# Windowed attention and a feed-forward layer on one core: TensorE in program order, one piece of weights converted per step, and the first loads in another order

## The chip, the cores and the metric

The kernel runs on one core of one Trainium2 chip. The metric is the device time of one execution in microseconds (us), from the first to the last instruction and what lies around them; the kernel before took 915.77 us as the median of three runs (915.74 to 917.31). A profile is one such execution taken by the hardware profiler, and its times count from the start of the span.

## What is computed

Eight batches of eight heads attend over 576 positions with a head dimension of 64. Heads 0 to 3 see the 32 positions that end at their own (the plain window), heads 4 to 7 see 32 positions that are four apart (the dilated window). The 4608 rows of 512 that this gives go through a feed-forward layer with 2048 inner columns. Everything is in float32.

```
scores = q @ k^T / sqrt(64), outside the window -1e9
attn   = exp(scores - max) / (sum + 1e-9)
x      = (attn @ v), heads side by side      # 4608 x 512
h      = x @ w_in                            # 512 x 2048
g      = h * clip(h + 3, 0, 6) / 6
out    = g @ w_out                           # 2048 x 512
```

## The kernel before

**The feed-forward layer** is cut into 12 chunks `c` of 384 rows and 16 slices `f` of 128 inner columns, so there are 192 steps (c, f). To keep the accuracy of float32, each matrix is split into a high and a low part (`xh` and `xl`, `gh` and `gl`, two parts of each weight in `wt`), and a product is three matmuls: high by high, high by low, low by high. The *first product* of a step (`gemm1`, lines 407 to 409) is 12 matmuls of 128x384 into one of two buffers `ps_h`. ScalarE (L412) and VectorE (L413) make g of it, ScalarE rounds it to its high part `gh` (L416), and VectorE subtracts that to get the low part `gl` (L417). The *second product* (`gemm2`, lines 428 to 430) is 9 matmuls of 128x512 into three accumulators `ps_o`; it belongs to the step two earlier (`LAG`). The accumulators are three of the six buffers `ps_a`, and the attention has the other three from the first second product on.

The steps do not run chunk by chunk from the start: they begin with (0,0) to (0,3), then alternate between chunk 0 and chunk 1, (0,4), (1,0), (0,5), (1,1) and so on, and from chunk 2 on they go chunk by chunk. Step 5 is therefore (1,0), the first to need rows of chunk 1.

**The attention** is done in 48 *trios*, each a group of blocks of 32 queries that fills 128 rows. The first 12 (`NFIRST`) run in rounds `tau` = 0 to 15, written in `first_items`: round tau does the scores of trio tau with the values of trio tau-3 mixed among them (`st_both`, on TensorE L228, L163 and L173), turns (transposes on TensorE, L242, and a copy on ScalarE, L247) the exponentials `e` of trio tau-1 and the result `x` of trio tau-4, and splits the latter into `xh` (ScalarE, L299) and `xl` (GpSimd, L302). The softmax is VectorE's (L195 and the lines around it) and so is the normalising by the sum (`z`, L207 and L208). From trio 9 on the values are single 32x65 matmuls that the trace shows in groups. The other 36 trios are set beside steps of the layer by a table (`beside`).

**The weights** come as 32 pieces, two per slice f (one of w_in, one of w_out), in 512 KB each (L323). They are 64-bit words and have to be put together to float32 on the chip in three stages, and one piece passes one stage per *beat* (`convert_beat`): *fields* (ScalarE twice, L338 and L339, VectorE L340), *join* (VectorE L346 and L350, then ScalarE's cast to the high part, L351) and *split* (VectorE L355 for the low part). A beat does the split of piece p-2, the join of piece p-1 and the fields of piece p. The beats ahead of the steps are set by the table `CB`, which lists the rounds in which one is run. From step 4 to step 29 (`LEAD` to `BEATS`) `step_at` runs one beat per step, and at even steps (`EXTRA` = 2) a second one at the end of the step.

**The loads** of q, k, v and the weights all stand on SP's queue, in the order in which they are written at the end of the function. `WITH` says how many pieces of weights are asked for after the loads of each round. The first nine trios have their loads in buffers of the weights' pool (18 buffers), the later ones in a pool of three, so that these wait for the trio three before. ScalarE's queue has the loads of the results out; GpSimd issues none.

**The order of the work.** `turn_of` gives what follows it a priority, in steps of the layer, and a scheduler orders the instructions of each engine by that and by what it thinks each will take. The order in which TensorE does the products, the small matmuls of the attention and the turns is therefore the scheduler's, and differs from the order in which the code is written. The lines that count most are:

```
        turn_of(n + 0.4)
        if LEAD <= n < BEATS:
            convert_beat()
        turn_of(n + G2)
        if n >= LAG:
            gemm2(*steps[n - LAG])
        ...
        turn_of(n + 0.9)
        if LEAD <= n < BEATS and n % EXTRA == 0:
            convert_beat()
```

Of the kernel before, what the change touches and what calls it, by code (L numbers as in the profile page):

```python
# [23 lines left out]
SPARE = 2  # L24
WORK = 12
BEATS = 30
EXTRA = 2
WARM = 8
ONV = ()
AHEAD = 3  # L30
LEAD = 4
NFIRST = 12
NLOAD = 3
NWIDE = 9
WITH = (0, 0, 0, 0, 2, 0, 2, 0, 2, 2, 2, 2)
CB = (6, 6, 7, 7, 8, 8, 9, 9, 10, 10, 11, 11, 12, 12)
BASE = 8
CD = 0.5
EARLY = (8, 9, 10, 11, 12, 13, 14, 15, 15)
# [7 lines left out]
def windowed_attention_ffn(ctx: ExitStack, tc: tile.TileContext, qk, vp, w, mask, out):  # L47
# [79 lines left out]
    def load_tile(t, name, at, n):  # L127

        if t >= NWIDE:
            return loads.tile([P, n], F32, name=name, tag=name)  # L130
        if t not in wide:
            wide[t] = wpool.tile([P, 4, DM], F32, name="first", tag="w").rearrange("p a n -> p (a n)")
        return wide[t][:, at : at + n]

    def load_qk(t):
        if t < T and t not in kqs:
            kqs[t] = load_tile(t, "kq", 0, KW + CH)
            nc.sync.dma_start(out=kqs[t], in_=qk[t].rearrange("h d x -> (h d) x"))

    def load_v(t):  # L140
        if t < T and t not in vs:
            v = load_tile(t, "v", KW + CH, TB * W)
            vs[t] = v.rearrange("p (n x) -> p n x", x=W)
            nc.sync.dma_start(out=v, in_=vp[t].rearrange("h k x -> (h k) x"))
# [176 lines left out]
    def load_w(p):  # L321
        st = wpool.tile([P, 4, WN], F32, name="st", tag="w")
        pace(nc.sync.dma_start(  # L323
            out=st[:, 0:2].rearrange("p a n -> p (a n)").bitcast(U32), in_=w[p // 2, p % 2].bitcast(U32)
        ))
        staged[p] = st
# [7 lines left out]
    def cv_fields(p):  # L334
        if p % 2 == 0:
            wt[p // 2] = wpool.tile([P, 4, WN], F32R, name="wt", tag="w")
        hi_w, lo_w, v, a, _, _ = parts(p)
        pace(nc.scalar.mul(v, hi_w, 2.0**-112))  # L338
        pace(nc.scalar.mul(a.bitcast(U32), lo_w.bitcast(U32), 2.0**-29))  # L339
        nc.vector.tensor_scalar(  # L340
            out=v.bitcast(U32), in0=v.bitcast(U32), scalar1=3, scalar2=None, op0=ALU.logical_shift_left
        )

    def cv_join(p):
        hi_w, _, v, a, hi, _ = parts(p)
        nc.vector.scalar_tensor_tensor(  # L346
            out=v.bitcast(U32), in0=hi_w.bitcast(U32), scalar=0x80000000, in1=v.bitcast(U32),
            op0=ALU.bitwise_and, op1=ALU.bitwise_or,
        )
        nc.vector.tensor_tensor(out=v.bitcast(U32), in0=v.bitcast(U32), in1=a.bitcast(U32), op=ALU.add)  # L350
        nc.scalar.copy(hi, v)  # L351

    def cv_split(p):
        _, _, v, _, hi, lo = parts(p)
        nc.vector.tensor_tensor(out=lo, in0=v, in1=hi.bitcast(F32), op=ALU.subtract)  # L355
        del staged[p]
# [5 lines left out]
    def load_ahead(n):  # L362
        while beat["loaded"] < min(n, NP):
            f = beat["fields"] // 2
            if len(staged) + f + 1 + 1 > NF + SPARE and len(staged) > 0 and beat["loaded"] >= 2:
                break
            load_w(beat["loaded"])
            beat["loaded"] += 1

    def convert_beat():  # L370
        if beat["split"] < beat["join"]:
            cv_split(beat["split"])
            beat["split"] += 1
        if beat["join"] < beat["fields"]:
            cv_join(beat["join"])
            beat["join"] += 1
        p = beat["fields"]
        if p < NP:
            load_ahead(p + 1)
            if p < beat["loaded"]:  # L380
                cv_fields(p)
                beat["fields"] += 1
        load_ahead(p + AHEAD)
# [10 lines left out]
    def turn_of(n):  # L394
        tc.cur_priority = max(first[0] + int(n * STEP), 0) + 1000

    def gemm1(n, c, f):
        last["g"] = True
        weights_ready(f)
        assert all(x in written for x in trios if c in chunks(*x))  # L400
        read[c] += 1
        r0 = (c * CH) % (2 * S)
        ph = ps_h.tile([P, CH], F32, name="ps_h")
        for kt in range(NK):
            a, b = xh[:, kt, r0 : r0 + CH], xl[:, kt, r0 : r0 + CH]
            ks = slice(kt * P, (kt + 1) * P)
            nc.tensor.matmul(ph, lhsT=wt[f][:, 0, ks], rhs=a, start=(kt == 0), stop=False)  # L407
            nc.tensor.matmul(ph, lhsT=wt[f][:, 0, ks], rhs=b, start=False, stop=False)  # L408
            last["pe"] = nc.tensor.matmul(ph, lhsT=wt[f][:, 1, ks], rhs=a, start=False, stop=(kt == NK - 1))  # L409
        turn_of(n + EV)  # L410
        t = work_tile("t")
        nc.scalar.activation(t, ph, AF.Relu, bias=three, scale=1.0)  # L412
        nc.vector.scalar_tensor_tensor(out=t, in0=t, scalar=6.0, in1=ph, op0=ALU.min, op1=ALU.mult)  # L413
        gh = work_tile("gh", F32R)
        gl = work_tile("gl", F32R)
        nc.scalar.copy(gh, t)  # L416
        nc.vector.tensor_tensor(out=gl, in0=t, in1=gh.bitcast(F32), op=ALU.subtract)  # L417
        gs[c, f] = gh, gl

    def gemm2(c, f):  # L420
        gh, gl = gs.pop((c, f))
        if f == 0:
            po[c] = [ps_a.tile([P, DM], F32, name="ps_o", tag="ps_a") for _ in range(TT)]
        if f == NF - 1:
            o = wpool.tile([P, TT, DM], F32, name="o", tag="w")
        for tt in range(TT):
            ts = slice(tt * P, (tt + 1) * P)
            nc.tensor.matmul(po[c][tt], lhsT=gh[:, ts], rhs=wt[f][:, 2], start=(f == 0), stop=False)  # L428
            nc.tensor.matmul(po[c][tt], lhsT=gh[:, ts], rhs=wt[f][:, 3], start=False, stop=False)  # L429
            last["pe"] = nc.tensor.matmul(po[c][tt], lhsT=gl[:, ts], rhs=wt[f][:, 2], start=False, stop=(f == NF - 1))  # L430
            if f == NF - 1:
                nc.scalar.mul(o[:, tt], po[c][tt], 1.0 / 6.0)
                r = c * CH + tt * P
                nc.scalar.dma_start(out=out[r : r + P, :], in_=o[:, tt])
# [31 lines left out]
    for i, p in enumerate(at):  # L466
        t = NFIRST + i
# [7 lines left out]
    def step_at(n):  # L475
        c, f = steps[n] if n < len(steps) else (None, None)
        turn_of(n)
        if c is not None:
            gemm1(n, c, f)
        turn_of(n + DEL)  # L480
        for step in beside.get((c, f, 0), []):
            step()
# [6 lines that stand above are left out]
        turn_of(n + DEL + 0.5)  # L489
        for step in beside.get((c, f, 1), []):  # L490
            step()
        turn_of(n + 0.9)
        if LEAD <= n < BEATS and n % EXTRA == 0:
            convert_beat()

    first[0] = BASE * STEP
    some = P + 2 * CH
# [3 lines left out]
    load_qk(1)  # L501
    load_qk(2)
    nc.sync.dma_start(out=mi[:, some:], in_=mask[:, some:])
    load_v(0)
    for t in range(3, NFIRST + 2):
        if t < NFIRST:
            load_qk(t)
        load_v(t - 2)
        load_ahead(sum(WITH[: t - 1]))
    n = 0  # L510
    for tau in range(NFIRST + 4):
        turn_of(tau - BASE)
        first_items(tau)
        turn_of(tau - BASE + CD)
        for _ in range(CB.count(tau)):
            convert_beat()
        for _ in range(EARLY.count(tau)):
            step_at(n)
            n += 1
    while n < len(steps) + LAG:  # L520
        step_at(n)
        n += 1
# [92 lines left out]
```

## Time and profile before

| what | value |
|---|---|
| median of three runs | 915.77 us (915.74 to 917.31) |
| the profiled execution | 915.34 us |
| its span, first to last instruction | 913.6 us (1.7 us lie around it) |
| mean granted TensorE clock | 0.991 |
| TensorE busy | 891.0 us, 98% |
| VectorE busy | 444.0 us, 49% |
| ScalarE busy | 346.5 us, 38% |
| GpSimd busy | 62.5 us, 7% |
| chain that ended last | TensorE 92%, DMA 4%, VectorE 2% |

A share is taken over the whole span, and says nothing of a single stage: the stages before and after 96 us differ, as the windows in the prediction show. In the rows below, PE is TensorE, DVE is VectorE, ACT is ScalarE, POOL is GpSimd and SP is the engine that issues the loads. A row of the timeline has the start, the duration, the engine, the line, the operation, the tile written and those read, and the shapes; in brackets stands an idle time ahead of it and what ended it. A row of waits has the total, the number and the longest.

### The profile page before, as it was taken

What the parts mean: (1) busy time and instruction counts of PE and PEld (TensorE: products, weight loads), DVE (VectorE), ACT (ScalarE), POOL (GpSimd) and SP (SyncE); (2) the same over time, 40 slices, a digit from 0 to 9 for tenths busy, and PEclk for the clock granted to TensorE, in tenths of its full rate; (3) what the DMA queues carried; (4) which work ended last, traced back from release to release, by engine and by line L of the source; (5) the groups of instructions that cost most, each with busy time, mean ns of one, the idle gap of its engine ahead of it and who ended that gap; (6) DMA issues with size and microseconds to landing.
All of it is one profiled execution on the core that took longest, in us unless ns stands there. A gap on an engine that the chain in (4) does not pass through costs nothing.

```text
span 913.6 us, 20574 instructions
## 1 busy us (share of the span) xinstructions
PE 891.0 (98%) x8732; PEld 791.6 (87%) x8732; DVE 444.0 (49%) x934; ACT 346.5 (38%) x661; POOL 62.5 (7%) x77
## 2 busy tenths in 40 slices
PE   6897999999999999999999999999999999999998
PEld 4576999989889899899888989988888998899996
DVE  3899983244545454444454445445444544422221
ACT  2778862333333333233333223233333332332322
POOL 0212100000010110000000000000100010000000
PEclk9799999999999999999999999999999999999999
DMA  9927430022313222222122123113211310100000
GB/s 354 386 83 260 140 93 0 1 95 89 86 54 119 72 70 81 66 67 84 47 85 85 48 64 104 51 46 99 71 49 52 116 32 11 45 5 1 36 1 34
DMA packets 37820, 74.87 MB, mean 82 GB/s; under 512 B 7264, under 2 KB 16608, under 8 KB 37728
## 3 DMA queue, kind: packets, MB, share of 16 engines
q1 hardware_dynamic: 32544, 64.12, 21.8%
q10 hardware_dynamic: 5184, 9.44, 2.7%
q8 instruction: 68, 1.11, 0.5%
q14 instruction: 24, 0.20, 0.1%
HBM read 57.02 MB, written 9.44 MB: 73 GB/s over the span
## 4 chain that ended last, share of the span: by engine, by line
PE 92%; DMA 4%; DVE 2%; ACT 1%; issue 0%; SPq 0%; POOL 0%
PE ps_o L428 15%; PE ps_h L407 15%; PE ps_h L409 14%; PE ps_h L408 14%; PE ps_o L429 14%; PE ps_o L430 14%; PE ps_a L181 3%; PE ps_a L163 2%; DMA first<-in_v 2%; DMA st<-in_w 1%; DMA v<-in_v 1%; DVE st L350 1%; DVE st L346 1%; DVE wt L355 0%; PE ps_a L242 0%
## 5 line engine op out<-in xcount | busy, mean ns | idle before, releaser
L413 DVE SCALAR_TENSOR_TENSOR t<-t,ps_h 128x384 f32<-128x384 f32 x192 | 106.3, 554 | 326.0 <-ACT t L412 325.8
L407 PE MATMUL ps_h<-xh,wt 128*128 128x384 f32 x768 | 261.5, 341 | 2.9 <-DVE t L413 2.8
L408 PE MATMUL ps_h<-xl,wt 128*128 128x384 f32 x768 | 259.9, 338 | 0.5 <-POOL xl L302 0.5
L409 PE MATMUL ps_h<-xh,wt 128*128 128x384 f32 x768 | 259.9, 338 | 0.0
L428 PE MATMUL ps_o<-wt,gh 128*128 128x512 f32 x576 | 228.7, 397 | 2.0 <-ACT gh L416 2.0
L429 PE MATMUL ps_o<-wt,gh 128*128 128x512 f32 x576 | 224.9, 390 | 0.0
L430 PE MATMUL ps_o<-wt,gl 128*128 128x512 f32 x576 | 221.3, 391 | 0.6 <-DVE gl L417 0.6
L412 ACT ACTIVATE t<-ps_h,three 128x384 f32<-128x384 f32 x192 | 111.1, 579 | 273.3 <-PE ps_h L409 273.0
L417 DVE TENSOR_TENSOR gl<-t,gh 128x384 fp32r<-128x384 f32 x192 | 107.0, 557 | 101.4 <-ACT gh L416 100.1
L407 PEld LDWEIGHTS ps_h<-xh,wt 128*128 128x128 f32 x768 | 144.9, 189 | 11.8 <-DVE t L413 3.3
L408 PEld LDWEIGHTS ps_h<-xl,wt 128*128 128x128 f32 x768 | 144.9, 189 | 8.7 <-POOL xl L302 0.6
L409 PEld LDWEIGHTS ps_h<-xh,wt 128*128 128x128 f32 x768 | 145.0, 189 | 0.8 <-issue 0.3
L416 ACT CAST gh<-t 128x384 fp32r<-128x384 f32 x192 | 98.5, 513 | 111.3 <-DVE t L413 109.1
L430 PEld LDWEIGHTS ps_o<-wt,gl 128*128 128x128 f32 x576 | 108.2, 188 | 24.2 <-DVE gl L417 1.0
L428 PEld LDWEIGHTS ps_o<-wt,gh 128*128 128x128 f32 x576 | 108.3, 188 | 20.1 <-ACT gh L416 2.3
L429 PEld LDWEIGHTS ps_o<-wt,gh 128*128 128x128 f32 x576 | 108.4, 188 | 15.7
L302 POOL TENSOR_TENSOR xl<-xf,xh 128x384 fp32r<-128x384 f32 (+3 forms) x72 | 62.2, 877 | 740.6 <-ACT xh L299 671.8
L200 ACT ACTIVATE e<-e 128x384 f32<-128x384 f32 x48 | 25.2, 526 | 112.4 <-DVE e L196 112.3
L163 PE MATMUL ps_a<-kq 64*32 64x64 f32 x1872 | 47.1, 225 | 0.0
L299 ACT CAST xh<-xf 128x384 fp32r<-128x384 f32 (+3 forms) x72 | 33.7, 536 | 34.7 <-DMA xf<-xf_t 34.6
L181 PEld LDWEIGHTS ps_a<-v,a 64*32 64x32 f32 x1728 | 35.8, 105 | 9.2 <-issue 8.6
L181 PE MATMUL ps_a<-v,a 64*32 64x65 f32 x1728 | 41.6, 225 | 0.0
(45 smaller groups left out, 494.6 us busy)
## 6 DMA issues: line engine op xcount, KB each, us to landing
st<-in_w SPq DMA_DIRECT2D x32, 512.0 KB, 5.7
kq<-in_qk SPq DMA_DIRECT2D x39, 416.0 KB, 4.5
v<-in_v SPq DMA_DIRECT2D x39, 390.0 KB, 3.5
out<-o ACTq DMA_DIRECT2D x36, 256.0 KB, 2.9
first<-in_qk SPq DMA_DIRECT2D x9, 416.0 KB, 8.0
first<-in_v SPq DMA_DIRECT2D x9, 390.0 KB, 8.5
a<-a_t SPq DMA_DIRECT2D x144, 24.0 KB, 1.8
xf<-xf_t SPq DMA_DIRECT2D x144, 24.0 KB, 1.8
```

Of the source, the lines that this page charges most:

```text
L163: last["pe"] = nc.tensor.matmul(ps[at : at + QB, 2 * QB * i : 2 * QB * (i + 1)], lhsT=x[rows, KW + QB * n : KW + QB * (n + 1)], rhs=x[rows ...
L181: last["pe"] = nc.tensor.matmul(ps[at : at + QB, i * W : (i + 1) * W], lhsT=ats[t][rows, QB * n : QB * (n + 1)], rhs=vs[t][rows, n, :], st ...
L407: nc.tensor.matmul(ph, lhsT=wt[f][:, 0, ks], rhs=a, start=(kt == 0), stop=False)
L408: nc.tensor.matmul(ph, lhsT=wt[f][:, 0, ks], rhs=b, start=False, stop=False)
L409: last["pe"] = nc.tensor.matmul(ph, lhsT=wt[f][:, 1, ks], rhs=a, start=False, stop=(kt == NK - 1))
L412: nc.scalar.activation(t, ph, AF.Relu, bias=three, scale=1.0)
L413: nc.vector.scalar_tensor_tensor(out=t, in0=t, scalar=6.0, in1=ph, op0=ALU.min, op1=ALU.mult)
L416: nc.scalar.copy(gh, t)
L417: nc.vector.tensor_tensor(out=gl, in0=t, in1=gh.bitcast(F32), op=ALU.subtract)
L428: nc.tensor.matmul(po[c][tt], lhsT=gh[:, ts], rhs=wt[f][:, 2], start=(f == 0), stop=False)
L429: nc.tensor.matmul(po[c][tt], lhsT=gh[:, ts], rhs=wt[f][:, 3], start=False, stop=False)
L430: last["pe"] = nc.tensor.matmul(po[c][tt], lhsT=gl[:, ts], rhs=wt[f][:, 2], start=False, stop=(f == NF - 1))
```

## The change

Four things are changed. TensorE's instructions are issued in the order in which the program writes them, while the other engines stay with the scheduler (`manual_schedule`). The second beat at even steps is gone, so one piece is converted per step; the table `CB` has 13 beats and no longer 14 ahead of the steps, one less in round 6. The loads of the first trios are in another order: q and k of trio 3 come ahead of the first values, and from there the values are loaded one round later against q and k than before. The weights stand behind loads of later trios: the first two pieces came behind the q and k of trio 6 and the values of trio 4, and now come behind those of trio 8 and 5; ten pieces are asked for ahead of the rounds, where it was twelve.

```
-EXTRA = 2
-WITH = (0, 0, 0, 0, 2, 0, 2, 0, 2, 2, 2, 2)
-CB = (6, 6, 7, 7, 8, 8, 9, 9, 10, 10, 11, 11, 12, 12)
+WITH = (0, 0, 0, 0, 0, 2, 0, 0, 2, 2, 2, 2)
+CB = (6, 7, 7, 8, 8, 9, 9, 10, 10, 11, 11, 12, 12)
...
         turn_of(n + 0.9)
-        if LEAD <= n < BEATS and n % EXTRA == 0:
-            convert_beat()
...
     nc.sync.dma_start(out=mi[:, some:], in_=mask[:, some:])
+    load_qk(3)
     load_v(0)
-    for t in range(3, NFIRST + 2):
+    for t in range(4, NFIRST + 3):
         if t < NFIRST:
             load_qk(t)
-        load_v(t - 2)
-        load_ahead(sum(WITH[: t - 1]))
+        load_v(t - 3)
+        load_ahead(sum(WITH[: t - 2]))
...
     with tile.TileContext(nc, schedule_with_timeline_sim=True) as tc:
-        windowed_attention_ffn(tc, *args, o)
+        with tc.manual_schedule(engines={mybir.EngineType.PE}):
+            windowed_attention_ffn(tc, *args, o)
```

Since one line of constants is gone, a line of the changed kernel has a number one lower than before (L407 becomes L406), up to the steps.

The following rows are the order in which each engine's instructions stand in the program. A name ends in a number of the build, which differs between the two kernels; `x3` is a group of three.

The first place is TensorE in round 8. L228 (after: L227) begins the scores of trio 8 with its mask, L163 (L162) are single blocks of scores, L173 (L172) single blocks of the values of trio 5, L242 (L241) the turns of the trios before, and 407 to 409 (406 to 408) are the first product of step 0. Before:

```order
L242 MATMUL ps_a_629<-ident_79,e_537 128x128 x3
L242 MATMUL ps_a_635<-ident_79,x_535 128x128 x3
L228 LDWEIGHTS mi_78
L228 MATMUL ps_a_660<-mi_78 128x384
L407 MATMUL ps_h_752<-xh_76,wt_558 128x384
L173 MATMUL ps_a_661<-first_109,a_546 32x65
L408 MATMUL ps_h_752<-xl_77,wt_558 128x384
L163 MATMUL ps_a_660<-first_122 32x64
L409 MATMUL ps_h_752<-xh_76,wt_558 128x384
```

The same place after, from the turns of round 8 to the mask of round 9:

```order
L241 MATMUL ps_a_712<-ident_81,e_616 128x128 x3
L241 MATMUL ps_a_718<-ident_81,x_614 128x128 x3
L406 MATMUL ps_h_743<-xh_78,wt_556 128x384
L407 MATMUL ps_h_743<-xl_79,wt_556 128x384
L408 MATMUL ps_h_743<-xh_78,wt_556 128x384
...
L227 LDWEIGHTS mi_80
L227 MATMUL ps_a_763<-mi_80 128x384
L172 MATMUL ps_a_764<-first_113,a_625 32x65
L162 MATMUL ps_a_763<-kq_126 32x64
```

The products of step 0 stood singly between the blocks of round 8, and now stand in one run of twelve behind all of round 8, ahead of the mask of round 9.

The second place is TensorE at step 5, (1,0), the first that reads rows of chunk 1, and so the split of trio 9 (its turn reads `x_1163` before and `x_1156` after; trio 10's reads `x_1278` and `x_1261`). Before, from the turn of trio 9 on, with the rest of trio 11's values (`a_1171`), the first product of step 6 (`ps_h_1371`) and one second product; step 5's own buffer is `ps_h_1292`:

```order
L242 MATMUL ps_a_1282<-ident_79,x_1163 128x128 x3
L173 MATMUL ps_a_1331<-v_153,a_1171 32x65 x17
L407 MATMUL ps_h_1371<-xh_76,wt_1091 128x384
...
L173 MATMUL ps_a_1331<-v_153,a_1171 32x65 x7
L428 MATMUL ps_o_996<-wt_965,gh_1218 128x512
...
L407 MATMUL ps_h_1292<-xh_76,wt_558 128x384
L242 MATMUL ps_a_1363<-ident_79,x_1278 128x128 x3
L408 MATMUL ps_h_1292<-xl_77,wt_558 128x384
```

After, with step 5 in `ps_h_1275` and step 6 in `ps_h_1354`:

```order
L241 MATMUL ps_a_1265<-ident_81,x_1156 128x128 x3
L406 MATMUL ps_h_1275<-xh_78,wt_556 128x384
L407 MATMUL ps_h_1275<-xl_79,wt_556 128x384
...
L427 MATMUL ps_o_989<-wt_851,gh_1115 128x512
...
L172 MATMUL ps_a_1314<-v_151,a_1164 32x65 x24
L241 MATMUL ps_a_1346<-ident_81,x_1261 128x128 x3
L406 MATMUL ps_h_1354<-xh_78,wt_1093 128x384
```

Between the turn of trio 9 and step 5's last products there stood trio 11's values, step 6's first product and a second product; now step 5 follows the turn directly, and all of those stand behind it.

The third place is VectorE at steps 7 and 8: L413 and L417 (L412 and L416) belong to the products, the other rows to the conversion (`st` is a piece on its way, `wt` its result, the ISA row is L350's addition). Before, from step 7's L413 to step 8's:

```order
L413 SCALAR_TENSOR_TENSOR t_1440<-t_1440,ps_h_1427 128x384
L350 ISA st_1398<-st_1398 128x1024
L355 TENSOR_TENSOR wt_1413<-st_1320,wt_1413 128x512
L340 TENSOR_SCALAR st_1417<-st_1417 128x512
L346 SCALAR_TENSOR_TENSOR st_1417<-st_1417 128x512
L417 TENSOR_TENSOR gl_1444<-t_1440,gh_1443 128x384
L340 TENSOR_SCALAR st_1454<-st_1454 128x512
L350 ISA st_1417<-st_1417 128x1024
L346 SCALAR_TENSOR_TENSOR st_1454<-st_1454 128x512
L355 TENSOR_TENSOR wt_1413<-st_1398,wt_1413 128x512
L413 SCALAR_TENSOR_TENSOR t_1481<-t_1481,ps_h_1468 128x384
```

After, between the same two operations:

```order
L412 SCALAR_TENSOR_TENSOR t_1413<-t_1413,ps_h_1400 128x384
L339 TENSOR_SCALAR st_1381<-st_1381 128x512
L345 SCALAR_TENSOR_TENSOR st_1381<-st_1381 128x512
L416 TENSOR_TENSOR gl_1417<-t_1413,gh_1416 128x384
L349 ISA st_1381<-st_1381 128x1024
L412 SCALAR_TENSOR_TENSOR t_1455<-t_1455,ps_h_1442 128x384
```

Eight operations of the conversion stood between them, and now three do.

## The prediction

> **What bounds the kernel now.** I read the page first, then busy time by stage, then the waits of the first 100 us, then single rows of the timeline. The page's head gives the span, against which everything is summed:
>
> ```profile
> span 913.6 us, 20574 instructions
> ```
>
> The stages come from the table of windows (per engine: busy us and instructions; then the granted TensorE clock, the DMA share and GB/s):
>
> ```profile
> 34.00:41.00 7.00, 7.00 (x99) 4.00 (x99) 6.73 (x12) 4.51 (x10) 2.12 (x3) 0.50 1.03 406
> 41.00:51.00 10.00, 9.39 (x146) 6.53 (x134) 7.53 (x16) 7.13 (x15) 1.97 (x2) 0.89 0.39 152
> 51.00:60.00 9.00, 9.00 (x131) 6.93 (x132) 9.00 (x22) 9.00 (x20) 1.13 (x1) 1.00 0.32 92
> 60.00:70.00 10.00, 10.00 (x142) 8.80 (x141) 10.00 (x20) 6.32 (x13) 1.41 (x1) 1.00 0.45 128
> 70.00:80.00 10.00, 7.47 (x125) 5.42 (x123) 9.60 (x19) 9.35 (x20) 2.04 (x2) 1.00 0.62 224
> 80.00:93.00 13.00, 10.18 (x92) 8.90 (x91) 13.00 (x27) 10.64 (x22) 4.66 (x5) 0.93 0.87 312
> 93.00:96.00 3.00, 3.00 (x14) 2.60 (x13) 2.97 (x7) 2.49 (x6) 0.88 (x1) 0.75 0.59 180
> 96.00:909.00 813.00, 813.00 (x7339) 733.00 (x7338) 369.76 (x782) 281.44 (x533) 44.40 (x55) 1.00 0.19 59
> ```
>
> From 96 us on TensorE (first column) is busy without a hole at the full clock, and VectorE (third) is busy for 370 of 813 us. So that stretch is TensorE's own work, and the change leaves the number of its products alone. Before 96 us TensorE has holes, and from 51 us VectorE is the full engine. The waits of the first 100 us (total, times, longest):
>
> ```profile
> PE ps_a L173 <- issue: 9.3, 4, 3.8
> ...
> ACT wt L351 <- DVE st L350: 8.3, 9, 2.1
> ...
> PE ps_h L407 <- DVE t L413: 2.8, 1, 2.8
> ...
> PE ps_o L428 <- ACT gh L416: 2.0, 1, 2.0
> ```
>
> TensorE's largest wait, 9.3 us, is put down to issue and not to data. It lies in the attention rounds before 33 us, where the change keeps TensorE's order, so I leave it. ScalarE and VectorE wait for each other inside the conversion of the weights (L351 after L350), and TensorE waits for the work after a first product (L413, L416).
>
> So the whole question is when the eighth first product (step 7) ends, since from there TensorE has all that it needs. Before, that is 93.12 us:
>
> ```profile
> 93.12 0.85 PE L242 MATMUL ps_a<-ident,x 128*128 128x128 f32 x3
> 93.61 0.78 PE L428 MATMUL ps_o<-wt,gh 128*128 128x512 f32 x1
> ...
> 95.48 0.34 PE L407 MATMUL ps_h<-xh,wt 128*128 128x384 f32 x1
> ```
>
> The last trio's turn (0.49 us) is still to come there, and after the change it stands ahead of that point. The six products from 93.61 to 95.48 take 1.87 us instead of two thirds of 2.04, so 0.51 us more than they would at the full clock. The time to beat is therefore 93.12 + 0.49 + 0.51 = **94.1 us**. The steady lengths are differences of starts:
>
> ```profile
> 102.38 0.39 PE L428 MATMUL ps_o<-wt,gh 128*128 128x512 f32 x1
> ...
> 104.42 0.34 PE L407 MATMUL ps_h<-xh,wt 128*128 128x384 f32 x1
> ...
> 106.50 0.39 PE L428 MATMUL ps_o<-wt,gh 128*128 128x512 f32 x1
> ```
>
> A second product of nine takes 2.04 us, a first product of twelve 2.08.
>
> **What the change does to TensorE at trio 8.** Before, six products of step 0 stand between the small ones of the attention:
>
> ```profile
> 35.24 0.69 PE L408 MATMUL ps_h<-xl,wt 128*128 128x384 f32 x1
> 35.86 0.42 PE L163 MATMUL ps_a<-first 64*32 64x64 f32 x2
> 36.21 0.69 PE L409 MATMUL ps_h<-xh,wt 128*128 128x384 f32 x1
> ```
>
> One product and its two small neighbours take 0.97 us here, at half the clock. Six of them are 5.8 us, against 1.04 us for six in a row later. After the change they stand behind the attention of the trio, so its scores are ready up to 4.8 us sooner. How much of this VectorE can use, its own rows say:
>
> ```profile
> 43.10 0.16 DVE L207 TENSOR_SCALAR z<-ps_a 128x6 f32<-128x6 f32 x1
> 43.17 0.55 DVE L195 TENSOR_REDUCE mx<-ps_a 128x6 f32<-128x384 f32 x1
> 43.64 0.42 DVE L340 TENSOR_SCALAR st<-st 128x512 uint32<-128x512 uint32 x1
> 43.97 0.69 DVE L350 CUSTOM_DVE_ANT_0 st<-st 128x1024 uint16<-128x1024 uint16 x1
> ...
> 79.74 0.54 DVE L413 SCALAR_TENSOR_TENSOR t<-t,ps_h 128x384 f32<-128x384 f32 x1
> 80.20 0.68 DVE L355 TENSOR_TENSOR wt<-st,wt 128x512 fp32r<-128x512 f32 x1
> 80.80 1.19 DVE L350 CUSTOM_DVE_ANT_0 st<-st 128x1024 uint16<-128x1024 uint16 x1
> ```
>
> From start to start, an operation on 384 columns takes 0.47 us (43.17 to 43.64), one of the conversion's L346, L350, L355 0.60 (80.20 to 80.80), L340 0.33, L207 and L208 together some 0.18. Ahead of trio 8's L207 at 43.10 the changed order has five rows less (two L355, one each of L340, L346, L350): 4 x 0.60 + 0.33 = 2.7. I put that point at 43.1 - 2.7 = **40.4 us**.
>
> **One piece per step.** From there I follow VectorE to the second operation of the fourteenth piece's join, because ScalarE's queue has that piece's cast (L351) ahead of the copy of trio 9, and in program order TensorE stands at step 5 until trio 9's low part is there. Counted in the order, this is 22 operations of 0.47, 31 of 0.60, 10 of 0.33 and five pairs of 0.18: 10.3 + 18.6 + 3.3 + 0.9 = 33.1 us. Before, the stretch from 43.10 to the L413 at 79.74 holds 21, 29, 10 and five of them, 31.5 us, and took 36.6: waits and stretching add 5.1 us. I take the same 5.1 for after. It can be nothing, if the new order brings no waits, and it can be more:
>
> ```profile
> L350 DVE CUSTOM_DVE_ANT_0 st<-st x16: 678/683/1504, 44.0 to 96.9; 128x1024 uint16<-128x1024 uint16 x16
> ```
>
> The median of 16 is 683 ns and the longest 1504, so single operations are stretched by up to 0.8 us. (The Trainium skill, page SBUF — State Buffer, section Who interferes with whom, says that VectorE with two SBUF inputs and GpSimd exclude each other for a whole instruction. This trace bears out the longest row and not the rule's full size, as the median stays at 683 ns. By the rule, GpSimd's 4.66 us in the window from 80 us would be lost whole, some 2 us more than I charge, and the sum would end above 916.)
>
> VectorE is then at 40.4 + 33.1 + 5.1 = 78.6 us. The chain behind it is in the trace of before for the same trio:
>
> ```profile
> 82.03 0.62 ACT L351 CAST wt<-st 128x512 fp32r<-128x512 f32 x1 [0.72 <-DVE st L350]
> ...
> 82.56 0.47 ACT L247 COPY xf<-ps_a 128x384 f32<-128x384 f32 x1
> ...
> 83.51 2.15 POOL L302 TENSOR_TENSOR xl<-xf,xh 128x96 fp32r<-128x96 f32 x2 [0.95 <-ACT xh L299]
> ...
> 85.64 0.34 PE L407 MATMUL ps_h<-xh,wt 128*128 128x384 f32 x1
> ```
>
> From the cast to the product that follows it is 3.6 us, so step 5 goes on at 82.2. Before, the order put trio 11's values, step 6's first product and a second product into this wait. In program order all of that stands behind it. The values of a trio and a turn take:
>
> ```profile
> 78.76 0.94 PE L173 MATMUL ps_a<-v,a 64*32 64x65 f32 x48
> 79.63 0.55 PE L242 MATMUL ps_a<-ident,x 128*128 128x128 f32 x3
> 80.11 0.75 PE L173 MATMUL ps_a<-v,a 64*32 64x65 f32 x34
> ```
>
> 0.87 and 0.48 us. Still to run are five products of step 5 (0.87), two second products (4.08), the values (0.87), two turns (0.96) and two first products (4.16): 10.9 us. Step 7 then ends at 82.2 + 10.9 = **93.1 us**, 1.0 us before the 94.1 of now. The profiled execution took 915.3 us, which is 913.6 of span and 1.7 around it, so the sum is 914.3. The median of the runs shown is 0.4 above that execution, which makes **914.8 us**.
>
> **Terms at nothing.** The first weights come later in SP's queue, behind loads of trios 7 and 8, and two fewer pieces (ten) are asked for ahead of the rounds; the eleventh then waits behind the loads of trios 12 and 13, which wait for trio 10's scores.
>
> ```profile
> L338 ACT ACTIVATE st<-st 128x512 f32<-128x512 f32 x16 | 10.9, 679 | 0.2 <-DMA st<-in_w 0.2
> ```
>
> ```profile
> st<-in_w SPq DMA_DIRECT2D x32, 512.0 KB, 5.7
> kq<-in_qk SPq DMA_DIRECT2D x39, 416.0 KB, 4.5
> ```
>
> Between 43 and 97 us the 16 conversions' first operations waited 0.2 us in all for a load, so loads have slack. Scores of trio 10 end near 52 us by the rates above and ScalarE wants the eleventh piece near 61; the 5.7 us of a load lie between, with some 3 to spare. Without that cover each microsecond is one on VectorE's list. After step 8, one piece per step is 0.33 + 3 x 0.60 = 2.1 us on VectorE, and 0.93 for L413 and L417, against 4.12 of TensorE: 1.1 us spare per step. The conversion lasts until step 24, and step 26 is the first to need its end. The tail is unchanged, as is the attention from trio 12 on, which stands within one product group of where it was.
>
> **Rivals.** *VectorE's waits go (faster).* If the 5.1 us are an artefact of the old order, step 7 ends at 88.0 and the time is 909.7. For it speaks that ScalarE's 8.3 us for L350 are waits between two orders that fitted badly; against it, that the new order has casts behind joins just as closely.
>
> *TensorE stands still in program order and falls to half clock (slower).* The places are the turn of trio 7 in round 11 (three of the six accumulators are the second product's, so this turn takes the one that trio 10's turn leaves, behind its copy on ScalarE) and step 5's wait for trio 9. The window from 80 us has the clock at 0.93 of 13 us and the next at 0.75 of 3: 1.8 + 1.5 = 3.3 us at half, so 1.65 us lost by one dip, after the single idle time of 2.8 us. Two such dips give 914.8 + 3.3 = 918.1. It decides from an idle time of about 2.8 us in one piece, and my sum leaves two to three at step 5. (The Trainium skill, page TensorE: Matmul & The Clock Gate, section Why this matters for your kernels, wants no idle gap over some 3 us, since a window of idling halves the clock. The trace agrees: 0.50 from 34 to 41 us. By it step 5 is a borderline case.)
>
> *The change does not do what it says.* The printed order shows that it does; I give this nothing.
>
> **How the numbers follow.** The forecast case (within 2 us of 914.8) has 0.42, of which 0.10 lies over 0.2% faster, 0.27 within and 0.05 over 0.2% slower; the faster rival 0.30; the slower one 0.28. A measurement of this kernel can tell 0.2%, 1.8 us, from no change. So faster is 0.40, same 0.27, slower 0.33. The range runs from a little beyond the faster rival, 908.5, to the slower one with late loads or full exclusion on top (2 us), 920.
>
> **What would show it.** Right: TensorE's products of step 0 in one run, about 1.04 us at full clock or 2 at half; step 7's end at 92 to 95 us; the longest wait of TensorE after 50 us on L301 (GpSimd) at step 5; the part from 96 us on unchanged to 0.5 us. Wrong: a hole in TensorE after 96 us, a wait of ScalarE for in_w over 1 us, or VectorE's L412 of step 7 before 88 or after 97 us.

## The result and the profile after

The changed kernel takes 917.21 us (median of 20 runs, 915.66 to 919.08) against 915.89 us before (20 runs, 912.98 to 917.42). The ratio is 1.0015 with a 95% interval of 1.0008 to 1.0022: it is slower by 0.15%, where the forecast was 0.1% faster. The profiled execution took 917.24 us, 1.9 us more than that of before.

The head of its page and the same stretches as before (busy us and instructions of TensorE, its weight loads, VectorE, ScalarE, GpSimd; then the granted clock, the DMA share and GB/s):

```profile
span 915.4 us, 20575 instructions
```

```profile
34.00:41.00 7.00, 4.92 (x111) 4.00 (x110) 6.93 (x14) 5.65 (x13) 2.25 (x3) 0.74 1.03 402
41.00:51.00 10.00, 6.27 (x111) 4.64 (x110) 7.95 (x16) 6.06 (x13) 1.69 (x2) 0.55 0.17 63
51.00:60.00 9.00, 8.59 (x139) 7.82 (x138) 9.00 (x22) 8.82 (x19) 1.39 (x1) 1.00 0.48 154
60.00:70.00 10.00, 5.32 (x113) 4.55 (x112) 10.00 (x20) 6.85 (x15) 1.76 (x2) 0.85 0.73 254
70.00:80.00 10.00, 10.00 (x139) 8.54 (x138) 9.38 (x18) 8.28 (x17) 3.75 (x4) 0.98 0.28 95
80.00:93.00 13.00, 10.87 (x95) 9.21 (x92) 10.33 (x20) 7.65 (x15) 3.13 (x4) 0.87 0.49 159
93.00:96.00 3.00, 3.00 (x18) 2.71 (x17) 2.83 (x7) 2.94 (x7) 0.00 (x0) 1.00 0.96 326
96.00:909.00 813.00, 812.39 (x7341) 733.02 (x7341) 377.41 (x792) 284.94 (x540) 44.30 (x55) 1.00 0.20 62
```

Two readings matter. From 96 us on TensorE has the same work at the full clock as before, but for a hole of 0.6 us (a wait for a load, at 217.6 us); VectorE's 7.7 us more there cost nothing that shows. Ahead of that TensorE now has its holes elsewhere: it was full from 51 to 70 us, and now stands for 4.7 us between 60 and 70. VectorE is full from 51 to 70 us as before, but no longer from 80 to 93 (10.33 of 13).

The waits of the first 100 us (total, times, longest):

```profile
PE ps_a L172 <- issue: 10.3, 4, 4.0
...
ACT wt L350 <- DVE st L349: 8.5, 7, 2.1
...
PE ps_a L241 <- ACT a L244: 4.7, 1, 4.7
PE ps_h L406 <- ACT xh L298: 4.6, 2, 3.1
...
PE ps_h L407 <- POOL xl L301: 1.3, 2, 0.6
```

The waits for L413 and L416, 4.8 us in all, are gone. In their place TensorE waits for the copy of a turn (L244) and for the two parts of x (L298, L301). ScalarE's wait for VectorE in the conversion (8.3 us, now 8.5) has stayed. Single rows of the timeline show where:

```profile
38.34 0.21 PE L172 MATMUL ps_a<-first,a 64*32 64x65 f32 x1 [1.96 <-issue]
...
41.26 0.16 DVE L206 TENSOR_SCALAR z<-ps_a 128x6 f32<-128x6 f32 x1
...
67.13 0.90 PE L241 MATMUL ps_a<-ident,x 128*128 128x128 f32 x3 [4.68 <-ACT a L244]
...
80.38 0.72 DVE L349 CUSTOM_DVE_ANT_0 st<-st 128x1024 uint16<-128x1024 uint16 x1
...
81.66 0.47 ACT L246 COPY xf<-ps_a 128x384 f32<-128x384 f32 x1
...
83.10 0.45 PE L406 MATMUL ps_h<-xh,wt 128*128 128x384 f32 x1 [1.51 <-ACT xh L298]
84.17 0.69 PE L407 MATMUL ps_h<-xl,wt 128*128 128x384 f32 x1 [0.62 <-POOL xl L301]
...
86.36 0.63 PE L428 MATMUL ps_o<-wt,gh 128*128 128x512 f32 x1
...
96.69 0.39 PE L427 MATMUL ps_o<-wt,gh 128*128 128x512 f32 x1
...
911.34 0.39 PE L429 MATMUL ps_o<-wt,gl 128*128 128x512 f32 x1
```

Step 5 waits for trio 9 from 81.6 to 84.2 us, and goes on at half clock: a product of 512 columns takes 0.63 us there and 0.39 later. Step 7 ends at 96.69, not at 93.1. The row to keep in mind is trio 9's copy, at 81.66: in the kernel before the same copy (L247) stood at 82.56. **The value for which everything waited comes 0.9 us sooner than before, and yet the kernel is slower.** From that copy to the end of the last product it took 909.01 - 82.56 = 826.5 us before (the last three products are one row, `908.17 0.84`), and takes 911.73 - 81.66 = 830.1 us now.

The end of the page was taken as unchanged. It is 0.9 us shorter: 915.4 - 911.7 = 3.7 us from the last product to the end, where it was 913.6 - 909.0 = 4.6.

### The profile page after: what moved, and what is told of

Its sections match the earlier page's. It is cut to its first block, busy times and chain, and to the rows that moved or that the text cites. A ratio compares the mean times of both kernels' runs of the same rounds, so it can differ in the third digit from the quotient of the medians.

```text
span 915.4 us, 20575 instructions
## 1 busy us (share of the span) xinstructions
PE 886.6 (97%) x8732; PEld 792.2 (87%) x8732; DVE 447.8 (49%) x934; ACT 346.2 (38%) x661; POOL 61.7 (7%) x77
## 4 chain that ended last, share of the span: by engine, by line
PE 91%; DVE 4%; ACT 1%; issue 1%; DMA 1%; SPq 0%; POOL 0%; DVEq 0%
PE ps_o L427 15%; PE ps_h L406 14%; PE ps_h L407 14%; PE ps_h L408 14%; PE ps_o L429 14%; PE ps_o L428 14%; PE ps_a L180 3%; PE ps_a L162 2%; DVE st L349 1%; DVE st L345 1%; DMA first<-in_v 1%; DVE wt L354 1%; DVE st L339 1%; PE ps_a L172 0%; PE ps_a L241 0%
## 5 line engine op out<-in xcount | busy, mean ns | idle before, releaser
L406 PE MATMUL ps_h<-xh,wt 128*128 128x384 f32 x768 | 262.3, 342 | 4.6 <-ACT xh L298 4.6
L412 DVE SCALAR_TENSOR_TENSOR t<-t,ps_h 128x384 f32<-128x384 f32 x192 | 106.4, 554 | 323.1 <-ACT t L411 323.1
L407 PE MATMUL ps_h<-xl,wt 128*128 128x384 f32 x768 | 260.1, 339 | 1.3 <-POOL xl L301 1.3
L429 PE MATMUL ps_o<-wt,gl 128*128 128x512 f32 x576 | 224.7, 390 | 0.0
L416 DVE TENSOR_TENSOR gl<-t,gh 128x384 fp32r<-128x384 f32 x192 | 107.1, 558 | 101.9 <-ACT gh L415 101.2
L406 PEld LDWEIGHTS ps_h<-xh,wt 128*128 128x128 f32 x768 | 145.5, 189 | 13.0 <-ACT xh L298 5.4
L407 PEld LDWEIGHTS ps_h<-xl,wt 128*128 128x128 f32 x768 | 145.6, 190 | 8.8 <-POOL xl L301 1.9
L301 POOL TENSOR_TENSOR xl<-xf,xh 128x384 fp32r<-128x384 f32 (+3 forms) x72 | 61.4, 864 | 744.2 <-ACT xh L298 743.6
L298 ACT CAST xh<-xf 128x384 fp32r<-128x384 f32 (+3 forms) x72 | 33.7, 534 | 36.5 <-DMA xf<-xf_t 36.2
L162 PE MATMUL ps_a<-kq 64*32 64x64 f32 x1872 | 46.4, 227 | 0.0
```

The source lines that it names most:

```text
L162: last["pe"] = nc.tensor.matmul(ps[at : at + QB, 2 * QB * i : 2 * QB * (i + 1)], lhsT=x[rows, KW + QB * n : KW + QB * (n + 1)], rhs=x[rows ...
```

## The experiments

Theory A was that program order costs the time, since TensorE stands behind a product whose inputs are not there, where the scheduler had put other work. Its rivals were the loads (B) and the conversions that now come later (C). The change is three edits, so the first five kernels are these edits by themselves and in pairs. Each has its ratio to the kernel before, run on the same chip. A difference in us between two of these kernels is one of their medians; the chips differ (the kernel before took 915.60 to 916.35 us on them), and by the ratios such a difference can come out up to 0.9 us other.

**e1: program order alone.**

```
+        with tc.manual_schedule(engines={mybir.EngineType.PE}):
+            windowed_attention_ffn(tc, *args, o)
```

> The kernel before with TensorE in program order, and nothing else changed (two pieces converted at even steps, the old loads). Theory A (the loss is TensorE standing behind a product whose inputs VectorE and ScalarE do not yet have, where the scheduler put other work): this alone is slower than before by 1 to 6 us, with idle times of TensorE over 1 us between 41 and 93 us and step 7 ending at 95 us or later. Theory B (the loss is the later place of the weights in SP's queue): within 1 us of before, as the loads are the old ones. Theory C (the loss is the one piece less converted early): within 1 us of before.

Measured: 918.32 us, ratio 1.0029 (1.0018 to 1.0041). TensorE's waits are at the places of the changed kernel, in round 11 (3.5 us, where the changed kernel has 4.7) and at step 5, where they are longer than there:

```profile
82.70 0.55 PE L407 MATMUL ps_h<-xh,wt 128*128 128x384 f32 x1 [2.04 <-ACT xh L299]
84.32 0.69 PE L408 MATMUL ps_h<-xl,wt 128*128 128x384 f32 x1 [1.07 <-POOL xl L302]
86.08 0.63 PE L428 MATMUL ps_o<-wt,gh 128*128 128x512 f32 x1
```

Theory A holds: 2.7 us slower than the 915.66 us of before on that chip, with the loads and the beats of before.

**e2: one piece per step alone** (the lines with EXTRA and the one number in CB).

> The kernel before with one piece converted per step and one beat less in round 6; TensorE's order is the scheduler's and the loads are the old ones. Theory A: within 1 us of before, or faster by up to 2 us, as VectorE has less to do before step 7 ends. Theory C: slower by 1 to 2 us. Theory B: within 1 us.

Measured: 913.31 us, ratio 0.9973 (0.9963 to 0.9984), so 2.4 us faster, a little more than was expected. Theory C falls, with the sign turned. Before, and in this kernel:

```profile
90.00 0.44 PE L407 MATMUL ps_h<-xh,wt 128*128 128x384 f32 x1 [2.82 <-DVE t L413]
```

```profile
89.85 0.45 PE L407 MATMUL ps_h<-xh,wt 128*128 128x384 f32 x1 [1.26 <-DVE t L413]
...
92.06 0.49 PE L242 MATMUL ps_a<-ident,x 128*128 128x128 f32 x3
```

With fewer conversions in VectorE's way, TensorE's wait for L413 ahead of step 7 falls from 2.82 to 1.26 us, and the half clock that followed it (the turn at 93.12 took 0.85 us, now 0.49) is gone.

**e3: the loads alone.**

> The kernel before with the new order of the loads alone. Theory B: slower by 1 to 2 us, with ScalarE's first conversion waiting for in_w. Theory A and theory C: within 1 us of before.

Measured: 916.63 us, ratio 1.0006 (0.9993 to 1.0018). Theory B isn't borne out; a cost of up to 0.18% isn't excluded.

**e4: program order and one piece per step.**

> The kernel before with TensorE in program order and one piece per step, but the old loads: the whole change without its loads. Theory A: as the whole change, 0.5 to 2.5 us slower than before, and faster than program order alone by 1 us or more, since fewer conversions stand ahead of trio 9's copy. Theory B: within 0.5 us of before, or faster. Theory C: as the whole change, and slower than program order alone.

Measured: 916.87 us, ratio 1.0017 (1.0005 to 1.0030), which is the changed kernel's 1.0015 without its loads, and 1.4 us faster than e1.

**e5: one piece per step and the loads, TensorE with the scheduler.**

> The changed kernel with TensorE's order given back to the scheduler: one piece per step and the new loads. Theory A (program order is what costs, the beats gain): 912 to 914.5 us, so 1 to 4 us faster than before. If the loads and the beats together cost what the whole change does: 916 us or more.

Measured: 913.82 us, ratio 0.9979 (0.9970 to 0.9988). With e2 this settles the sum: the beats bring some 2 us, the loads next to nothing, and program order on top of both costs 917.2 - 913.8 = 3.4 us. In the profile of e5 the copy of trio 9 stands here:

```profile
83.38 0.47 ACT L247 COPY xf<-ps_a 128x384 f32<-128x384 f32 x1
```

Its last product ends at 906.9, which is 823.5 us behind the copy, against 830.1 in program order. So in program order the copy comes 1.7 us sooner, 6.6 us more lie behind it, and 0.9 are given back at the end: 4.0 us, as the spans have it (911.4 and 915.4).

Which part of the 6.6 us is a loss in itself? Three theories were tried. H: every hole of TensorE is one. V: up to step 5 VectorE's list sets the time, and holes ahead of that cost nothing. D: what counts is the work of TensorE that stands behind the wait for trio 9 and could have been done inside it, and the half clock that follows.

**e6: the hole in round 11 filled.** The turns and splits of `first_items` become a function of their own, `first_turns`, and in rounds 9 to 12 it stands behind that round's step.

```
+BEHIND = (9, 10, 11, 12)
...
         first_items(tau)
+        if tau not in BEHIND:
+            first_turns(tau)
...
             step_at(n)
             n += 1
+        if tau in BEHIND:
+            turn_of(tau - BASE)
+            first_turns(tau)
```

> The changed kernel, still in program order, with the turns of rounds 9 to 12 written behind that round's step, so that the 4.7 us for which TensorE stood in the turns of round 11 have products to fill them. Theory H (each hole of TensorE is a loss in itself): 3 us or more faster than the changed kernel, 914 us or less. Theory V (up to step 5 the time is set by VectorE's list, so that a hole filled earlier only opens a longer one at step 5): within 1.5 us of the changed kernel's 917.2, with the wait at step 5 longer by the 4 us that are gained in round 11.

Measured: 918.9 us (twelve runs, 915.61 to 919.21), ratio 1.0025 (1.0015 to 1.0035), so no faster than the changed kernel. Theory H falls:

```profile
80.12 0.61 PE L242 MATMUL ps_a<-ident,x 128*128 128x128 f32 x3 [3.52 <-ACT a L245]
...
84.84 0.69 PE L408 MATMUL ps_h<-xl,wt 128*128 128x384 f32 x1 [0.66 <-POOL xl L302]
```

The hole has moved from round 11 to trio 9's turn, and step 5 goes on at 84.84 where it was 84.17. The work that was pulled forward is lost again at the next value that is late.

**e7: the split of pieces 4 to 13 on GpSimd.**

```
+ONPOOL = range(4, 14)
...
-        nc.vector.tensor_tensor(out=lo, in0=v, in1=hi.bitcast(F32), op=ALU.subtract)
+        eng = nc.gpsimd if p in ONPOOL else nc.vector
+        eng.tensor_tensor(out=lo, in0=v, in1=hi.bitcast(F32), op=ALU.subtract)
```

> The changed kernel with the split of pieces 4 to 13 on GpSimd in place of VectorE: ten operations of 0.6 us less on VectorE ahead of step 5. Theory V: the L349 ahead of trio 9's copy ends 4 to 6 us sooner and the time falls by 3 to 5 us, to 912 to 914. Theory H: the holes at the turns of round 11 and in step 0 stay, and the time falls by less than 1.5 us. If GpSimd and VectorE shut each other out for whole operations, VectorE's other rows grow by as much as was taken away and nothing is gained.

Measured: 922.95 us, ratio 1.0078 (1.0065 to 1.0091). The timeline:

```profile
82.06 4.70 POOL L356 TENSOR_TENSOR wt<-st,wt 128x512 fp32r<-128x512 f32 x3
...
88.99 0.69 PE L409 MATMUL ps_h<-xl,wt 128*128 128x384 f32 x1 [3.89 <-POOL xl L302]
```

This doesn't answer the question: three splits stood in GpSimd's queue ahead of trio 9's low part, and took 4.70 us. So it was tried again with earlier pieces.

**e10: the split of pieces 2 to 8 on GpSimd** (`ONPOOL = range(2, 9)` in the same edit).

> The changed kernel with the split of pieces 2 to 8 alone on GpSimd, so that none stands in GpSimd's queue right ahead of trio 9's low part, as three did when pieces 4 to 13 were moved. Theory V (VectorE's number of operations ahead of step 5 sets the time): seven operations of 0.6 us less, the time falls by 2 to 4 us. Rival (step 5 is set by the round trips between ScalarE, VectorE and TensorE, not by VectorE's number of operations): within 1 us of 917.2, with idle time on VectorE between 51 and 80 us.

Measured: 920.87 us, ratio 1.0046 (1.0029 to 1.0063), 3.7 us slower than the changed kernel, which neither side expected. VectorE has time to spare now (5.9 us of waits for ScalarE's L413), and two rows of VectorE and two of GpSimd say what it lost:

```profile
DVE t L414 <- ACT t L413: 5.9, 3, 3.9
...
PE ps_a L242 <- ACT a L245: 5.1, 1, 5.1
```

```profile
64.11 1.70 DVE L346 SCALAR_TENSOR_TENSOR st<-st 128x512 uint32<-128x512 uint32 x1
65.95 1.26 DVE L350 CUSTOM_DVE_ANT_0 st<-st 128x1024 uint16<-128x1024 uint16 x1
67.25 0.62 ACT L351 CAST wt<-st 128x512 fp32r<-128x512 f32 x1 [2.03 <-DVE st L350]
```

```profile
63.99 1.28 POOL L356 TENSOR_TENSOR wt<-st,wt 128x512 fp32r<-128x512 f32 x1 [4.05 <-ACT wt L351]
65.23 1.44 POOL L302 TENSOR_TENSOR xl<-xf,xh 128x384 fp32r<-128x384 f32 x1
```

VectorE's L346 begins at 64.11, GpSimd's split ends at 65.27, and L346 ends 0.54 us after that; L350 ends 0.54 us after GpSimd's next operation ends at 66.67. It looks as if each had waited for GpSimd's to end, and the cast behind them, with the copy of a turn behind that, is what TensorE stood for in round 11 (5.1 us, where it was 4.7). But this is a small part of the loss: TensorE came to that wait at 65.8 us, and in the changed kernel at 62.5, so most of it was lost before. Of that, 0.9 us were there by 34 us (the row of VectorE that starts at 33.48 in the changed kernel starts at 34.42), ahead of the first split on GpSimd at 42.35; the rest was not taken apart. Theory V as a count of VectorE's operations falls: seven fewer made it slower. What VectorE's list costs when nothing is given to GpSimd in its place isn't answered by this; e4, with fewer conversions than e1, was the faster one.

**e8: step 5's wait filled with idle products**, ten by zero weights that add nothing.

```
+FILL = 10
...
+    none = const.tile([P, P], BF16, name="none")
+    nc.gpsimd.memset(none, 0.0)
...
+            for _ in range(FILL if n == 5 and kt == 2 else 0):
+                nc.tensor.matmul(ph, lhsT=none, rhs=mi[:, P : P + CH], start=False, stop=False)
```

> The changed kernel with ten products by zero weights (they add nothing to the sum) written into the middle of step 5, where TensorE waits for trio 9: 1.7 us of work in a wait of 2.1. If the half clock after that wait is caused by the idle time there, step 5's last five products and the second product behind them run at the full clock and the time falls by 1 to 1.8 us. If the half clock comes from elsewhere, it stays and the time is the changed kernel's or up to 1 us more.

Measured: 916.09 us, ratio 1.0005 (0.9996 to 1.0015), 1.1 us faster than the changed kernel.

```profile
80.49 1.80 PE L408 MATMUL ps_h<-mi,none 128*128 128x384 bf16 x10
82.39 0.44 PE L411 MATMUL ps_h<-xh,wt 128*128 128x384 f32 x1
83.44 0.44 PE L412 MATMUL ps_h<-xl,wt 128*128 128x384 f32 x1 [0.61 <-POOL xl L304]
...
84.65 0.39 PE L433 MATMUL ps_o<-wt,gh 128*128 128x512 f32 x1
...
94.39 0.39 PE L432 MATMUL ps_o<-wt,gh 128*128 128x512 f32 x1
```

The second product behind step 5 runs at 0.39 us and not at 0.63: with the idle time filled, the half clock there doesn't come. From the first product behind the wait to the end of step 7 it takes 94.39 - 83.44 = 10.95 us, where the changed kernel took 12.5, so in the profile the half clock costs 1.6 us. In the medians it is 1.1 us, and that isn't clear of noise, as the interval overlaps the changed kernel's.

**e9: steps 5 and 6 exchanged**, so that (0,5), which reads no row of trio 9, stands ahead of (1,0).

```
+    steps[LEAD + 1], steps[LEAD + 2] = steps[LEAD + 2], steps[LEAD + 1]
```

> The changed kernel in program order, with steps 5 and 6 exchanged: (0,5), which reads no row of trio 9, is written ahead of (1,0), which does. Theory D (program order costs what TensorE has to do behind the wait for trio 9 and could have done inside it, and the half clock that follows): the 2.1 us of (0,5) fill the wait and no half clock follows, so the time falls by 2 to 4 us, to 913 to 915. If VectorE's list moves back by as much as TensorE's work comes forward (the two pieces for (0,5) are needed one step sooner), the time stays within 1 us of 917.2.

Measured: 913.84 us, ratio 0.9972 (0.9959 to 0.9985), 3.4 us faster than the changed kernel: all that program order had cost. The copy of trio 9 and the seventh product of (1,0), the first to read its rows, are followed by the wait in round 11 and the window:

```profile
82.22 0.47 ACT L246 COPY xf<-ps_a 128x384 f32<-128x384 f32 x1
...
88.16 0.34 PE L406 MATMUL ps_h<-xh,wt 128*128 128x384 f32 x1
```

```profile
PE ps_a L241 <- ACT a L244: 3.6, 1, 3.6
```

```profile
80.00:93.00 13.00, 13.00 (x158) 11.43 (x158) 12.61 (x24) 10.07 (x21) 5.45 (x5) 1.00 0.70 226
```

The copy comes 0.6 us later than in the changed kernel, and TensorE is busy for 13 of 13 us at the full clock: real work fills the wait. Theory D stands. The hole in round 11 is still there in this kernel (3.6 us), so it wasn't what program order lost.

**e11: one piece per step (e2) with the early splits on GpSimd.**

> The kernel before with one piece per step (913.3 us) and the split of pieces 2 to 8 on GpSimd: the candidate for a kernel that beats both. If VectorE's list is what holds it between 51 and 93 us: 910 to 912. If GpSimd's longer operation (1.3 us where VectorE takes 0.6) delays the weights or stretches VectorE's rows: 914 or more.

Measured: 916.15 us, ratio 0.9998 (0.9987 to 1.0009), so the splits on GpSimd cost e2 all its gain, under the scheduler too.

**e12: the edits of e9 and e6 together**, with round 13's turns behind its step as well.

> The changed kernel in program order with both edits: steps 5 and 6 exchanged, and the turns of rounds 9 to 13 written behind that round's step. Steps exchanged alone left an idle time of 3.6 us in round 11 and 2.6 us lost at half clock behind it. If these are a loss of their own once step 5 no longer waits: 2 to 4 us faster than with the steps exchanged alone (913.84), 910 to 912. If the last value needed from VectorE and ScalarE (trio 9's copy, for (1,0)) comes no sooner, TensorE stands there in place of round 11, and the time is 913 to 916.

Measured: 915.74 us, ratio 0.9997 (0.9988 to 1.0005), 1.9 us slower than e9. Its rows at (1,0):

```profile
84.46 0.52 PE L242 MATMUL ps_a<-ident,x 128*128 128x128 f32 x3 [2.07 <-DVE x L210]
...
88.42 0.69 PE L408 MATMUL ps_h<-xl,wt 128*128 128x384 f32 x1 [0.68 <-POOL xl L302]
```

As in e6, what was gained in round 11 is waited for again at trio 9, and the half clock comes back with it (0.69 us for a first product).

The fastest kernels measured are e2 (913.31), e5 (913.82) and e9 (913.84), all three faster than both kernels of the case.

## Why the prediction was wrong

The sum put step 7's end at 93.1 us, 3.6 us too soon. Its terms, one by one:

- **Trio 8's L207 at 40.4**: 41.26. The sum took 2.7 us off for five rows that are gone. Three of them lie ahead of 33.4 us, and there VectorE, done sooner, only waited longer for ScalarE. Before, and after:

```profile
33.42 0.56 DVE L340 TENSOR_SCALAR st<-st 128x512 uint32<-128x512 uint32 x1 [0.55 <-ACT st L338]
```

```profile
33.48 0.64 DVE L339 TENSOR_SCALAR st<-st 128x512 uint32<-128x512 uint32 x1 [1.35 <-ACT st L337]
```

  From that row on it took 43.10 - 33.42 = 9.7 us before and 41.26 - 33.48 = 7.8 after: the other two rows (1.2 us) are gone, and a wait of 0.7 for ScalarE. So 1.5 of the 2.7 us were not gained, and 0.7 came unforeseen. The step that failed is to count each row that is gone as time gained, also where VectorE then waits for ScalarE. TensorE's wait for issue was left out on the ground that it lies ahead of 33 us; one of these waits came at 38.34 and took 1.96 us, but VectorE is busy for 7.71 of those 7.78 us, so nothing shows that it reached VectorE.
- **VectorE's list, 33.1 us and 5.1 of waits and stretching**: from 41.26 to 81.10 (80.38 and 0.72) it took 39.8 us, so 6.7 of waits and stretching, 1.6 more than was charged. The list was right, the term mis-sized. The waits for ScalarE are 2.6 us, and were 2.4. The rows of VectorE that lie beside GpSimd's L301 (at 45.60, 55.96, 60.79, 70.23 and 78.90) are together 3.3 us longer than such rows take alone (0.68 us each), and those of before were 2.4; the other 0.5 us is small gaps. The clearest pair: GpSimd's L301 runs from 60.31 to 61.73, and VectorE's L354, begun at 60.79, ends at 62.29, 0.56 us after it. The Trainium skill (SBUF — State Buffer, Who interferes with whom) has VectorE contend with GpSimd, under an exclusive lock, when VectorE reads two inputs in SBUF. This pair agrees with it. The prediction charged too little for the stretching.

```profile
60.31 1.42 POOL L301 TENSOR_TENSOR xl<-xf,xh 128x384 fp32r<-128x384 f32 x1 [3.86 <-ACT xh L298]
```

```profile
60.79 1.50 DVE L354 TENSOR_TENSOR wt<-st,wt 128x512 fp32r<-128x512 f32 x1
```

- **From the cast to the product, 3.6 us**: 3.1 (81.10 to 84.17). Right within 0.5.
- **The work behind it, 10.9 us**: 12.5 (84.17 to 96.69). The list of what stands behind the wait was right, and e9 shows that it is what program order costs. It was priced at the full clock, and about 1.6 us went to half clock: in e8, without it, the same work took 10.95. The slower rival had this dip, but let it begin at 2.8 us of idle time in one piece; here 1.51 and 0.62 us with one product between them were enough, and in e8, where products fill it, the dip is gone.
- **The tail, unchanged**: 0.9 us shorter, as below. It hid a quarter of the miss.

Together 0.9 + 1.6 - 0.5 + 1.6 = 3.6 us at step 7, less 0.9 at the tail: 2.7 on the 914.3 of the sum is 917.0, and the profiled execution took 917.24. The mechanism was told rightly (step 5 held by trio 9's copy, all else behind it). The steps that failed are sizes: the 5.1 us of waits and stretching, taken over from the old order, were 6.7; the work behind step 5's wait, priced at the full clock at 10.9, took 12.5; and the start of VectorE's list was put 0.9 us too early. Each of these is as large as the gain of 1 us that the sum forecast, so its sign was not secure.

Of the rest: fewer beats do help (e2), the loads cost nothing that could be measured (e3), the stretch from 96 us on is unchanged but for 0.6 us. Six products of step 0 did run together, in 2.1 us at half clock; but TensorE's longest wait after 50 us is the 4.7 us in round 11 and not the one for L301 at step 5, and step 7's L412 starts at 97.9 us, which the prediction had named as a sign of being wrong. The faster rival, that VectorE's waits go with the old order, is wrong. The slower rival (918.1) came nearest. It named both places, the turn of trio 7 and step 5, and both showed; its price of one dip, 1.65 us, is what e8 gives for step 5's, and by e6 and e12 the wait in round 11 doesn't count beside it.

## What to carry to other kernels

When an engine is put into program order, look for the first instruction that waits for a slow chain, and count what stands behind it on the engine and needs nothing of that chain: that work is the price, and moving one such step ahead of the wait (e9) brought back all of it. A hole of the bound engine ahead of such a point was no loss here: filling it (e6, e12) moved the wait, and the kernel got no faster. Price the work behind a wait of a microsecond or two at the lower clock as well as at the full one, and count operations of VectorE that lie beside GpSimd's with the time until GpSimd's ends.

## What the runs showed of the hardware that was not expected

- **The tail goes with the order of the last nine products.** The scheduler had the last three products of all accumulators together at the end (before: one row of three from 908.17), while in program order each accumulator is finished by itself, so that ScalarE scales the first ones while the last is computed:

```profile
910.40 1.28 ACT L431 ACTIVATE o<-ps_o 128x512 f32<-128x512 f32 x2 [3.05 <-PE ps_o L429]
```

From the last product's end to the end of the span it took 3.7 to 3.8 us in every kernel in program order that was profiled, and 4.5 to 4.6 in every one with the scheduler. That the order alone makes the difference is argued and not shown: a kernel with e5's order and this end wasn't tried.

- **The clock after an idle time isn't given by its length alone.** At one and the same place, TensorE's wait for L416 near 76 us, an idle time of 1.97 us was followed by half clock in e2 and one of 1.95 us was not in e5. The two windows:

```profile
70.00:80.00 10.00, 8.03 (x79) 5.45 (x77) 8.89 (x18) 8.78 (x20) 2.08 (x2) 0.85 0.51 178
```

```profile
70.00:80.00 10.00, 7.53 (x108) 5.49 (x109) 8.98 (x18) 8.87 (x19) 2.09 (x2) 1.00 0.56 188
```

The Trainium skill (TensorE: Matmul & The Clock Gate, Why this matters for your kernels) asks for no idle gap over some 3 us. By these runs half clock can follow gaps of 1.5 to 2 us too, and what else decides it was not settled.
